# Loading two neighbouring tokens per piece in the first two batches of a gated-linear-attention and mixer kernel

## The chip, the cores and the metric

The kernel runs on one core of one Trainium2 chip. The metric is the device time of one launch in microseconds (us), the median over several runs.

A core has five engines that run side by side: TensorE (PE, matrix multiplies; its weight loads are shown as PEld), VectorE (DVE), ScalarE (ACT), GpSimd (POOL) and SyncE (SP, which here issues every transfer). They work on SBUF (128 partitions); PE writes its results to PSUM, which has eight banks of 128 x 512 fp32. Sixteen DMA engines carry data between HBM and SBUF. Each engine runs its own list of instructions in a fixed order, and semaphores make it wait for the others.

## What is computed

The reference chains two parts. The first is a recurrence with a gate per channel, for 4 batches, 8 heads, 768 tokens and head width 48:

```python
for t in range(S):
    state = alpha[:, :, t, :, None] * state + np.einsum('bhd,bhe->bhde', k[:, :, t], v[:, :, t])
    y[:, :, t] = np.einsum('bhd,bhde->bhe', q[:, :, t], state)
```

The heads of `y` are laid side by side to `x` (4 x 768 x 384), and a mixer follows: `U` is 768 x 32, `V` 32 x 768, `w_ch1` 384 x 1536 and `w_ch2` 1536 x 384.

```python
h = x.transpose(0, 2, 1) @ U @ V
u = x + h.transpose(0, 2, 1)
ch = np.maximum(u @ w_ch1, 0.0) @ w_ch2
return u + ch
```

Inputs and output are fp32 in HBM; the matmuls take bf16.

## The kernel before

**The recurrence in chunks.** A batch is cut into six chunks of 128 tokens. One chunk, all eight heads, is one call of `stage_gla` (L325). Tokens lie on the partitions. `stage_loads` (L313) brings four tiles of 128 x 8 x 48 fp32 for each chunk: alpha, k, q and v. In HBM a head's token is a row of 48 values, so that each load consists of 1024 pieces of 192 bytes:

```python
P.add({"SP": 1020.0}, lambda e: nc.sync.dma_start(t(), src[b, :, sl, :].rearrange("h t d -> t h d")), w=[t], prio=key)
```

Then, for each chunk:

- ScalarE takes the logarithm of alpha (`lt`, L331). PE multiplies it by an upper triangle of ones, which gives the prefix sums over the tokens (L338), and by a column of ones, which gives the totals (L341), with a mask added by `offd` (L339). ScalarE takes exp of minus, plus and total (`ai`, `aa`, `tot`, L349 to L351).
- `rk = k * ai` and `rq = q * aa` (L356, on POOL or DVE) are transposed by PE (L368) and copied from PSUM to `kT` and `qT`. `rv` is v in bf16.
- PE forms the scores of each head (L389, 48 rows of the array, so two heads at a time in 64-row tiles). VectorE multiplies them by the causal mask `maskc` into `pm` (L399).
- PE forms the state's increment `rk' rv` (L416). In the first batch PE also adds the state before, through an identity matrix (L414), and VectorE multiplies by `tot` (L427). In later batches VectorE adds (`sm`, L439), then POOL or VectorE multiplies.
- `y` is the state before seen through `qT` (L450) plus `pm' rv` (L452). It is copied to `xb`.

**The mixer.** After the six chunks of a batch, `stage_mix` (L461) forms `U' x` (L469) and from it `u = x + V' U' x` twice: as `uT`, with channels on the partitions (in the first batch directly, L488 and L491; later by transposing, L510), and as `ub`, with tokens on the partitions (L500 and the sum on VectorE, L501). `mlp1` (L525) multiplies `uT` by the first weights (L537, three matmuls for each of 24 tiles) with a relu (L547 on ACT, L549 on DVE). `mlp2` (L553) multiplies by the second weights (L560, twelve matmuls for each of 6 tiles), adds `ub` (L567) and stores (L568).

**What sets the order.** Nothing is ordered by hand. Every operation is handed to a planner (`Plan.add`) with an assumed cost for each engine that may do it, a priority and the tiles it reads and writes. `Plan.run` walks a clock of its own: at each step it takes, of the engines, the one that could start first, gives it the ready operation of lowest priority number, and hands out buffers and PSUM banks as they come free. The outcome is a fixed order for each engine. A `Buf` with a `reserve` takes a bank only when more than that many are free; `mlp1` and `mlp2` do so with 4 except in the last batch (L527, L554). `slack` is added to the time at which an operation counts as ready, and PE pays 95 ns in the plan for each change of tile mode. In the early part idle PE is given filler matmuls on zeros (L268), up to 33 us of the plan's clock.

Loads have priorities too. Chunk `kk`'s alpha, k and q have `kk`, `kk + 0.1` and `kk + 0.2`; v has `kk + 1.25`, that is behind alpha, k and q of the next chunk, except in the last chunk of a batch. The fp32 input ring `io` has 36 tiles; the 24 weight tiles pass through it too, twelve behind the loads of the first batch (priority 5.5) and twelve behind chunk 7 (7.9).

## Time and profile before

| What | Value |
|---|---|
| median of 5 runs | 181.38 us (180.14 to 182.75) |
| the profiled execution | 181.89 us, of which its span is 180.1 us |
| PE busy | 162.5 us (90% of the span) |
| DVE, ACT, POOL busy | 107.3, 103.4, 57.3 us |
| HBM read, written | 23.79 MB, 4.72 MB |
| DMA packets | 107603, of which 101408 under 512 bytes |
| loads of alpha, k, q, v | 24 each, 192 KB each, 3.7 to 3.9 us from issue to landing |
| weight loads | 24, 192 KB each, 4.4 us from issue to landing |

The span is the stretch from the first to the last recorded event of one execution. The profile page shows the busy share of each engine in 40 slices of the span; other views give the busy time in any stretch, the instructions in order of time with what each waited for, and the chain of work that ended last. A matmul's duration in the records (about 330 ns for 384 columns) includes the way through the array; matmuls that follow each other overlap, so that the pitch from one to the next is shorter.

### The profile page before, as it was taken

The numbers are of one execution on the slowest core, as the hardware profiler recorded it, in microseconds if no ns is written. First come the engines' busy times: TensorE is split into PE (matmuls) and PEld (weight loads), VectorE is DVE, ScalarE is ACT, GpSimd is POOL, SyncE is SP. The second block draws the span as 40 slices with busy tenths as digits, with TensorE's granted clock in tenths as the row PEclk, the third lists the DMA queues.
The fourth block names the chain that finished last, engine by engine and source line by source line (L and its number), as shares of the span: only waits on it lengthen the run. The fifth ranks groups of instructions, "written<-read, shape, count | busy, mean of one in ns | idle before, by whom it ended". The sixth has DMA issues, their size and how long they took to land.

```text
span 180.1 us, 4283 instructions
## 1 busy us (share of the span) xinstructions
PE 162.5 (90%) x1622; PEld 101.4 (56%) x1622; DVE 107.3 (60%) x209; ACT 103.4 (57%) x241; POOL 57.3 (32%) x90
## 2 busy tenths in 40 slices
PE   6778688889989998877999999999999999999992
PEld 2344455456556665454766576566665665665560
DVE  2486787969637895693789789376672822100331
ACT  4556558786775545693789759217867200897000
POOL 5432320225434664606584545424600000000000
PEclk9999999999999999996999999999999999999999
DMA  5999999999999998998999989881000023100222
GB/s 117 218 201 209 203 235 292 240 195 309 289 214 188 251 218 186 251 221 169 223 191 184 204 163 220 175 247 47 0 0 4 0 87 116 63 0 0 87 87 87
DMA packets 107603, 28.77 MB, mean 160 GB/s; under 512 B 101408, under 2 KB 107552, under 8 KB 107584
## 3 DMA queue, kind: packets, MB, share of 16 engines
q1 hardware_dynamic: 107584, 28.52, 69.6%
q8 instruction: 12, 0.20, 0.4%
q14 instruction: 7, 0.06, 0.1%
HBM read 23.79 MB, written 4.72 MB: 158 GB/s over the span
## 4 chain that ended last, share of the span: by engine, by line
PE 50%; SPq 16%; DMA 13%; issue 6%; DVE 5%; POOL 4%; ACT 4%; POOLq 0%; ACTq 0%
PE ps L560 20%; PE ps L537 19%; SPq L316 12%; DMA io<-in_alpha_dram 7%; DMA io<-in_moe_w_ch_dram 5%; SPq L294 3%; PE ps L368 3%; DMA out_dram<-ou 2%; DVE pm L399 2%; POOL rq L356 1%; POOL rk L356 1%; PE ps L452 1%; PE ps L338 1%; PE ps L389 1%; DVE rq L356 1%
## 5 line engine op out<-in xcount | busy, mean ns | idle before, releaser
L537 PE MATMUL ps<-uT,w_sb 128*128 128x384 bf16 x288 | 53.7, 331 | 0.4 <-ACT uT L275 0.4
L560 PE MATMUL ps<-w_sb,h1t 128*128 128x384 bf16 x288 | 50.1, 326 | 0.0
L547 ACT ACTIVATE h1t<-ps 128x384 bf16<-128x384 f32 x70 | 33.4, 490 | 21.3 <-PE ps L537 21.0
L560 PEld LDWEIGHTS <-h1t 128*128 128x128 bf16 x288 | 27.1, 98 | 16.5
L537 PEld LDWEIGHTS <-w_sb 128*128 128x128 bf16 x288 | 26.3, 98 | 16.3 <-issue 1.3
L399 DVE TENSOR_TENSOR pm<-ps,maskc 128x512 bf16<-128x512 f32 x48 | 31.0, 683 | 3.1 <-PE ps L389 3.1
L567 DVE TENSOR_TENSOR ou<-ub,ps 128x384 f32<-128x384 bf16 x24 | 13.3, 553 | 32.9 <-PE ps L560 31.3
L356 POOL TENSOR_TENSOR rk<-io,ai 128x384 bf16<-128x384 f32 x21 | 19.5, 928 | 24.9 <-ACT ai L349 22.2
L549 DVE TENSOR_SCALAR h1t<-ps 128x384 bf16<-128x384 f32 x26 | 13.8, 555 | 9.5 <-PE ps L537 9.4
L356 POOL TENSOR_TENSOR rq<-io,aa 128x384 bf16<-128x384 f32 x16 | 14.6, 913 | 8.5 <-PE ps L368 3.2
L331 ACT ACTIVATE lt<-io 128x384 bf16<-128x384 f32 x24 | 12.8, 532 | 7.4 <-DMA io<-in_alpha_dram 7.1
L349 ACT ACTIVATE ai<-ps 128x384 bf16<-128x384 f32 x24 | 12.0, 501 | 6.6 <-PE ps L341 4.9
L279 POOL CAST rv<-io 128x384 bf16<-128x384 f32 x18 | 9.8, 551 | 13.4 <-DMA io<-in_v_dram 10.0
L501 DVE TENSOR_TENSOR ub<-xb,ps 128x384 bf16<-128x384 bf16 x24 | 11.6, 548 | 3.1 <-PE ps L500 3.1
L368 PE MATMUL ps<-ident,rk 128*128 128x128 bf16 x96 | 9.6, 224 | 3.5 <-POOL rk L356 2.1
L350 ACT ACTIVATE aa<-ps 128x384 bf16<-128x384 f32 x24 | 12.1, 503 | 0.0
L268 PE MATMUL ps<-filler 128*128 128x512 bf16 x34 | 10.7, 423 | 1.2 <-DVE offd L235 1.2
L368 PE MATMUL ps<-ident,rq 128*128 128x128 bf16 x96 | 9.4, 220 | 2.3 <-POOL rq L356 1.9
L368 PEld LDWEIGHTS <-rk 128*128 128x128 bf16 x96 | 6.5, 100 | 8.0 <-POOL rk L356 4.3
L452 PE MATMUL ps<-rv,pm 128*128 128x48 bf16 x192 | 9.5, 185 | 1.6 <-DVE pm L399 1.6
L427 POOL TENSOR_TENSOR st<-sm,tot 128x384 bf16<-128x384 f32 x8 | 6.6, 829 | 13.3 <-DVE sm L439 13.3
L275 ACT COPY qt<-ps 128x512 bf16<-128x512 bf16 x12 | 7.1, 588 | 6.4 <-PE ps L368 4.8
(71 smaller groups left out, 198.3 us busy)
## 6 DMA issues: line engine op xcount, KB each, us to landing
io<-in_alpha_dram SPq DMA_DIRECT2D x24, 192.0 KB, 3.9
io<-in_k_dram SPq DMA_DIRECT2D x24, 192.0 KB, 3.9
io<-in_q_dram SPq DMA_DIRECT2D x24, 192.0 KB, 3.9
io<-in_v_dram SPq DMA_DIRECT2D x24, 192.0 KB, 3.7
io<-in_moe_w_ch_dram SPq DMA_DIRECT2D x24, 192.0 KB, 4.4
out_dram<-ou SPq DMA_DIRECT2D x24, 192.0 KB, 1.9
u_in<-in_moe_U_dram SPq DMA_DIRECT2D x1, 96.0 KB, 3.3
v_in<-in_moe_V_dram SPq DMA_DIRECT2D x1, 96.0 KB, 2.9
```

The source lines that it names most:

```text
L316: P.add({"SP": 1020.0}, lambda e: nc.sync.dma_start(t(), src[b, :, sl, :].rearrange("h t d -> t h d")), w=[t], prio=key)
L331: P.add({"ACT": 435}, lambda e: nc.scalar.activation(lt()[:, :, 0:D], at(), AF.Ln), r=[at], w=[lt], prio=pr + 40, slack=sl)
L349: P.add({"ACT": 390}, lambda e: nc.scalar.activation(ai().rearrange("t h d -> t (h d)"), cb()[:, 0:DM], AF.Exp, scale=-1.0), r=[cb], w=[ai ...
L350: P.add({"ACT": 390}, lambda e: nc.scalar.activation(aa().rearrange("t h d -> t (h d)"), cb()[:, 0:DM], AF.Exp), r=[cb], w=[aa], prio=pr + ...
L356: eng.tensor_tensor(dst()[:, :, 0:D], a(), x(), op=ALU.mult)
L368: nc.tensor.matmul(t[:, p, :], lhsT=ring()[:, 2 * p : 2 * p + 2, :].rearrange("t h w -> t (h w)"), rhs=ident, start=True, stop=True, is_tr ...
L399: nc.vector.tensor_tensor(pm()[:, :, par, :], s2, maskc.to_broadcast([C, HP, C]), op=ALU.mult)
L537: nc.tensor.matmul(hb()[:, 0:TW], lhsT=w1_sb[:, ct, jt * 128 : (jt + 1) * 128], rhs=uT()[:, ct, tt * TW : (tt + 1) * TW], start=(ct == 0), ...
L547: nc.scalar.activation(dst, hb()[:, 0:TW], AF.Relu)
L549: nc.vector.tensor_scalar_max(dst, hb()[:, 0:TW], 0.0)
L560: nc.tensor.matmul(hb()[:, 0:DM], lhsT=h1()[:, jt, c * C : (c + 1) * C], rhs=w2_sb[:, jt, :], start=(jt == 0), stop=(jt == NJ - 1),)
L567: P.add({"DVE": 468}, lambda e: nc.vector.tensor_tensor(ou(), ub()[:, c, :], hb()[:, 0:DM], op=ALU.add), r=[hb, (ub, c)], w=[ou], prio=-100)
```

## The change

Only batches 0 and 1 (`PAIR`) are treated in the new way. Their loads take two neighbouring tokens per piece: partition p of a tile holds tokens 2p and 2p+1 of a block of 256 tokens, for four of the eight heads. A load still has 192 KB, in 512 pieces of 384 bytes. A unit of work is then two chunks by four heads instead of one chunk by eight heads: partitions 0 to 63 belong to the first chunk of the block and 64 to 127 to the second, and a token's parity `j` takes the place of half of the heads in the free dimension. There are six units in a batch, as there were six chunks; two states run side by side, one for each half of the heads.

The new `stage_pair` does for a unit what `stage_gla` does for a chunk. The prefix sums take three matmuls (`upto` is the triangle within each chunk, `below` the same without its diagonal). The scores are 16 matmuls of 64 x 64 tiles, the state increments eight and the outputs sixteen matmuls in 64-row tiles. The copy of the transposed q puts the two parities back in the tokens' order. States, and the copies of y, are handled in halves of 192 columns. New constant tiles are built at the start.

Besides, in the whole kernel: `ub` of the first batch (L500, L501) has a later priority and reserves three banks; `mlp1` and `mlp2` reserve 2, 2, 2 and 0 banks; v of batches 2 and 3 has priority `kk + 0.3`; the plan's cost of a load is 720 or 900 instead of 1020; fillers end at 28 us of the plan's clock. `stage_gla` now serves batches 2 and 3 alone and loses its branches for the first two.

```diff
+    PAIR = (0, 1)
+    RES = (2, 2, 2, 0)
...
+    upto = const.tile([C, C], BF16, name="upto")
+    nc.vector.tensor_copy(upto, ut_ones)
+    nc.vector.memset(upto[0:64, 64:128], 0.0)
+    below = const.tile([C, C], BF16, name="below")
+    nc.vector.tensor_tensor(below, upto, ident, op=ALU.subtract)
+    mask2 = const.tile([C, 2, 2 * C], BF16, name="mask2")
+    nc.gpsimd.memset(mask2, 0.0)
+    nc.gpsimd.affine_select(
+        out=mask2, in_=mask2, compare_op=ALU.is_gt, fill=1.0, base=0, pattern=[[1, 2], [-1, 2 * C]], channel_multiplier=2
+    )
+    maskp = const.tile([C, 1, 2, C], BF16, name="maskp")
+    nc.vector.tensor_copy(maskp[0:64, 0], mask2[0:64, :, 0:C])
+    nc.vector.tensor_copy(maskp[64:128, 0], mask2[64:128, :, C : 2 * C])
...
-    P.warm_until = 33000.0
+    P.warm_until = 28000.0
...
+            if b in PAIR:
+                hs, sl = slice((c % 2) * HP, (c % 2 + 1) * HP), slice((c // 2) * 2 * C, (c // 2 + 1) * 2 * C)
+                P.add(
+                    {"SP": 720.0},
+                    lambda e: nc.sync.dma_start(
+                        t().rearrange("p (h j) d -> p h (j d)", j=2), src[b, hs, sl, :].rearrange("h (p j) d -> p h (j d)", j=2)
+                    ),
+                    w=[t], prio=key,
+                )
+                return
...
-            for t, src, o in ((at, alpha, 0.0), (kt, k, 0.1), (qt, q, 0.2), (vt, v, 1.25 if c < NC - 1 else 0.3)):
+            for t, src, o in ((at, alpha, 0.0), (kt, k, 0.1), (qt, q, 0.2), (vt, v, 1.25 if c < NC - 1 and b in PAIR else 0.3)):
...
+    def stage_pair(b, u, sprev, xb):
...
+        def f_cum(e):
+            l2 = jh(lt()[:, :, 0:D])
+            nc.tensor.matmul(cb()[:, 0:DM].rearrange("p (i h d) -> p i h d", i=2, d=D), lhsT=upto, rhs=l2[:, 0:1].to_broadcast([C, 2, HP, D]), start=True, stop=False)
+            nc.tensor.matmul(cb()[:, 0:Q], lhsT=below, rhs=l2[:, 1], start=False, stop=False)
+            nc.tensor.matmul(cb()[:, Q : 2 * Q], lhsT=upto, rhs=l2[:, 1], start=False, stop=False)
...
+        def f_ev(e, dst, tb, swap):
+            t = bf(tb())[:, 0:512].rearrange("x (a j m) -> x a j m", a=2, j=2)
+            d = dst().rearrange("x e c -> x (e c)")
+            d = d.rearrange("x (a m j) -> x a j m", a=2, j=2) if swap else d.rearrange("x (a j m) -> x a j m", a=2, j=2)
+            copy(e, d, t)
...
+        def f_sc(e):
+            for n in range(4):
+                a, j = n // 2, n % 2
+                for par in range(2):
+                    o = 64 * par
+                    for c in range(2):
+                        r = slice(64 * c, 64 * c + 64)
+                        nc.tensor.matmul(
+                            sc[par]()[r, n * C : (n + 1) * C],
+                            lhsT=kT()[o : o + D, n, r], rhs=qT()[o : o + D, 2 * a + c, :],
+                            start=(n == 0), stop=(n == 3), skip_group_check=True,
+                        )
+
+        P.add({"PE": mm(*[C] * 4)}, f_sc, r=[kT, qT], w=[sc[0], sc[1]], prio=pr + 10, mode="Q", slack=sl)
...
+        P.add({"PE": mm(*[2 * D] * 4)}, f_d, r=[rk, rv], w=db, prio=pr + 8, mode="H", slack=sl)
...
+        def f_y(e):
+            for h in range(HP):
+                for j in range(2):
+                    for c in range(2):
+                        r = slice(64 * c, 64 * c + 64)
+                        nc.tensor.matmul(
+                            yb[c]()[:, h * D : (h + 1) * D], lhsT=pm()[r, (h // 2) * 2 + j, h % 2, :], rhs=rv()[r, HP * j + h, :],
+                            start=(h == 0 and j == 0 and before[c] is None), stop=(h == HP - 1 and j == 1), skip_group_check=True,
+                        )
...
-            pr += 100.0
+            pr = mlp_prio(0, 0.3)
         for c in range(NC):
-            hb = Buf(bank)
+            hb = Buf(bank, 3 if b == 0 else 0)
...
-            hb = Buf(bank, 0 if b == B - 1 else 4)
+            hb = Buf(bank, RES[b])
...
-        st = None
+        st = [None, None]
         for c in range(NC):
-            st = stage_gla(b, c, st, xb)
+            if b in PAIR:
+                st[c % 2] = stage_pair(b, c, st[c % 2], xb)
+            else:
+                st[0] = stage_gla(b, c, st[0], xb)
```

## The prediction

> **What bounds the kernel now.** I read the busy rows of the page first, then the stretches between the events of the program, then the timeline at the places where TensorE (PE) waits.
>
> ```profile
> PE   6778688889989998877999999999999999999992
> PEclk9999999999999999996999999999999999999999
> DMA  5999999999999998998999989881000023100222
> ```
>
> Each digit is a slice of 4.5 us. The DMA engines are full up to slice 27 (122 us), when the last input has landed; PE has nines without a break from slice 19 (86 us) on. So two bounds follow one another, and both are full between 86 and 122 us. A busy PE is not a PE at its peak, so I count its work instead. The chain that ended last shows the pitch of one matmul where nothing waits:
>
> ```profile
> 142.16 11.05 PE ps L560 x68
> 153.21 11.70 PE ps L537 x72
> 164.91 11.71 PE ps L560 x72
> 120.09 0.33 PE ps L389 x8
> 120.42 1.41 PE ps L560 x8
> ```
>
> 11.70/72 gives 162.5 ns for a matmul of 384 columns (0.423 ns a column, so 56 ns for 128 columns, 42 for 96, 82 for 192). The eight score matmuls in 64-row mode (L389) cost 0.33 us plus 0.11 us by which the eight matmuls after them exceed 8 x 162.5 = 1.30: 0.44 us, of which 8 x 26 ns are matmuls and 0.23 us the way into the mode and back, so 0.115 us a switch. L452 (48 columns) takes 25 ns each (0.20 us for 8 in the same chain). With these prices the PE queue of the program before holds 146.4 us of work without the fillers of L268. The stretches:
>
> ```profile
> core 0: us, PE busy (x) PEld busy (x) DVE busy (x) ACT busy (x) POOL busy (x), PEclk, DMA share, GB/s
> 4.00:36.60 32.60, 25.09 (x296) 14.40 (x296) 24.36 (x46) 20.44 (x51) 8.51 (x11) 1.00 1.02 227
> 36.60:70.00 33.40, 32.41 (x346) 21.21 (x345) 23.29 (x43) 21.82 (x55) 15.58 (x23) 1.00 1.00 234
> 70.00:86.00 16.00, 12.10 (x145) 7.79 (x140) 10.49 (x21) 9.89 (x24) 6.77 (x9) 0.90 1.01 212
> 86.00:122.00 36.00, 35.70 (x407) 23.68 (x405) 28.44 (x53) 22.73 (x55) 18.85 (x25) 1.00 0.94 198
> 122.00:177.00 55.00, 54.48 (x433) 33.45 (x431) 19.55 (x37) 26.84 (x58) 5.18 (x6) 1.00 0.12 44
> ```
>
> Up to 36.66 us (first prefix-sum matmul of batch 1) my count of real PE work is 15.9 us: 20.8 us are idle or filler. From there to 70.07 us (the same matmul of batch 2) it is 32 us of 33.4. From 70 to 86 us it is 9.3 us of 16, and the clock drops. From 86.03 to 176.65 us, where the last matmul ends, it is 89.2 us of 90.6. So PE's own work sets the end, and what can be gained is its idle time before 86 us, which DMA causes:
>
> ```profile
> 69.50 0.52 ACT L331 ACTIVATE lt<-io 128x384 bf16<-128x384 f32 x1 [0.60 <-DMA io<-in_alpha_dram]
> 70.07 0.33 PE L338 MATMUL ps<-lt,ut_ones 128*128 128x384 bf16 x1
> 81.65 0.51 POOL L279 CAST rv<-io 128x384 bf16<-128x384 f32 x1 [4.70 <-DMA io<-in_v_dram]
> 82.21 0.29 PE L416 MATMUL ps<-rv,rk 128*128 128x96 bf16 x3 [1.99 <-POOL rv L279]
> ```
>
> The first load of batch 2 starts its chunk at 69.5 us; at 81.65 us a late v holds PE for 2 us, and the 90% clock of that stretch follows.
>
> **The change, part by part.**
>
> *Loads.* 48 of the 96 input loads move 512 pieces of 384 bytes in place of 1024 of 192. The price of a piece, from stretches of one kind:
>
> ```profile
> 4.00:24.00 20.00, 14.94 (x190) 8.63 (x191) 13.57 (x26) 11.33 (x30) 6.59 (x8) 1.00 1.06 206
> 26.00:34.00 8.00, 6.78 (x79) 4.21 (x80) 6.28 (x12) 6.32 (x15) 0.35 (x1) 1.00 0.99 296
> 41.00:49.00 8.00, 7.84 (x75) 4.82 (x74) 6.79 (x13) 5.29 (x14) 4.38 (x8) 1.00 0.96 306
> ```
>
> 192 KB at 206 GB/s is 0.954 us for a load in 192-byte pieces; at 300 GB/s it is 0.655 us in the weights' 1536-byte pieces. The trace has no 384-byte piece. Bounds: 0.954 (no gain) and 0.655. A straight line through the two, per piece and engine (14.9 and 82 ns), gives 24.5 ns x 32 = 0.784 us. A rule of the Trainium skill speaks against the change: "DMA: Bandwidth & Descriptors", section Specifications, asks for at least 512 bytes for line rate and says that below this the engine reads, modifies and writes; 384 is still below, which taken at its worst leaves 0.954. The same page, "How a descriptor splits into AXI transactions", has reads start at 256-byte boundaries: 192-byte pieces at multiples of 192 then fetch 9 beats of 32 bytes on average, 384-byte pieces 14, so 7 for each 192; with its 3 cycles a packet that is 12 against 8.5, an estimate of 0.676 us. I take 0.73, between line and page: 0.224 us x 48 = 10.75 us of DMA, half of it in batch 0. Under the 512-byte rule it is nothing. The SP queue has the same 148 instructions, but three output stores that stood ahead of the first load of batch 2 come later: 3 x 0.655 = 2.0 us. First load of batch 2: 69.5 - 12.75 = 56.8 us, and its prefix sum can run at 57.4.
>
> *v of the last two batches.* Its place goes from one chunk late to its own chunk. That removes the wait of 4.7 us at 81.65; it pulls each v ahead of the next chunk's alpha by one load (about 1 us), which costs nothing while DMA is ahead of PE, as it then is.
>
> *PE work of a pair unit* (12 units take the place of 12 chunks). Prefix sum: two more matmuls of 192 columns, +0.165 us. Scores: 16 of 64x64 in place of 8. The trace has no 64x64 tile; perfect overlap of four would be 14 ns each, the nearest row (L452) says 25 each, and I take 25: 0.40 against 0.21, +0.19. State increments: 8 of 64 rows at 25 against 4 at 42, +0.03. Outputs: 16 at 25 against 8, +0.20. Identity matmuls: 8 of 192 columns against 4 of 384, even. Switches: 96 in the whole queue against 59, 37 x 0.115 = 4.3 us. Sum: 12 x 0.585 + 4.3 = 11.3 us; PE's queue grows from 146.4 to 157.6. The "TensorEngine Tiling (Array Packing)" page of the skill, Restrictions, says that column tiling disables the fast weight load; by "TensorE: Matmul & The Clock Gate" (LDWEIGHTS) 64 columns then take 53 ns, so 0.85 us for 16 and +5.4 us over 12 units. The column-tiled loads that the trace has speak against it:
>
> ```profile
> 72.46 0.12 PEld L469 LDWEIGHTS <-u_sb 128*32 128x32 bf16 x6
> ```
>
> Six in 0.12 us. I stay with 25 ns; with the rule only the two score groups that stand behind the point below would show fully, +0.9 us.
>
> *Order: the first batch's sums later.* This decides what 11.3 us are worth. I counted the PE queue up to the first prefix sum of batch 2. Before: 47.8 us ahead of it, 98.6 behind, and all 72 second-layer matmuls of batch 0 (11.7 us) ahead. After: 43.8 ahead, 113.8 behind, and those 72 all behind. The pair units' extra work thus falls nearly all ahead of that point, beside loads that PE waits for anyway, and the work moved behind fills 70 to 86 us, where PE stood still. If that cover is gone, each us of it counts in full.
>
> *VectorE, ScalarE, GpSimd.* The swapped copy of q's transposes writes in steps of two elements; not in the trace: 0.42 us (plain copy on VectorE) to 0.68 (the masks' fp32 pass of 512), I take 0.60. State and y operations come in halves; a half has no row here, between 0.28 (half of 0.55) and 0.55, I take 0.35. The masks stay two of 0.64 (1.28 for two). VectorE's queue from batch 0's transposed sums to batch 1's last mask, at pitches of the timeline (1.49 us for 3 relus, 2.87 for 6 sums): 13 relus x 0.50, 12 masks x 0.64, 13 state halves x 0.35, 6 sums x 0.48, 4 scalings x 0.70, 3 swapped and 2 plain copies, 4 y halves: 28.4 us, some 25 ahead of the point. The densest stretch of the trace has VectorE busy 8.9 of 10 us, so 25 us need 28.1. ScalarE has less there. The new constants (a 128x512 select on GpSimd, about 4 x 0.29, then copies on VectorE) delay batch 0's first mask and padding by up to 1 us, beside loads.
>
> *Sum.* Batch 1's first prefix sum: 36.66 - 24 x 0.224 = 31.3 us. The first of batch 2 comes at the latest of three: PE 31.3 + (43.8 - 19.5 of work) = 55.6; DMA 57.4; VectorE 31.3 + 28.1 = 59.4. I take 58.5. Behind it 113.8 us, plus idle at the rate of today's dense part (1.4 in 89) 1.8: last matmul at 174.1 against 176.65, -2.55 us. The profiled execution took 181.89 us (span 180.1 and 1.8 around it), so 179.3; the median of the five runs, 181.38, lies 0.5 under it: 178.8 us.
>
> **Rivals.** (1) *VectorE becomes the bound in batch 1.* My sum leaves 27 us for batch 1 up to that point, with 25 us of VectorE work in them. Break-even is a first prefix sum of batch 2 at 61.05 us (176.65 - 115.6), 2.5 us behind my value. If VectorE reaches only the 79% of 86 to 122 us (28.44 of 36), 25 us take 31.6 and the point is 62.9, and a us more if the swapped copy waits too: 64, end at 179.6, +2.95, 184.3 us. For it: no stretch is denser than 89%. Against: ScalarE may take copies, and batch 0 ran at 75%. (2) *384 bytes are no cheaper* (the 512-byte rule): only 2 us of stores move, point at 68.1, end 183.7, 188.4 us. Against: the weights' 300 GB/s show that pieces cost. (3) *The loads run ahead but the gain is paid back*: point at 60.5 to 61.5, no change, 181.4. (4) *Loads at 0.68 and PE alone binding*: point at 56.2, end 171.8, 176.5 us.
>
> **How the numbers follow.** About 1% (1.8 us) is what a measurement of this kernel tells from no change. Chances: my forecast 0.45 (range 176.5 to 181, of it 0.09 within 1%), rival 4 0.14, rival 3 0.15, rival 1 0.19, rival 2 0.07. Faster 0.36 + 0.14 = 0.50, same 0.24, slower 0.26. The range, 175.5 to 184.5, leaves out rival 2 and the far ends of 1 and 4.
>
> **What would show it.** A load rate of 260 to 290 GB/s in the first 20 us (206: rival 2). The first prefix sum of batch 2 near 58 us and no PE gap of over 1 us after it; a VectorE busy above 8.5 of 10 between 31 and 60 with PE waiting for masks is rival 1. Score groups of 16 in about 0.6 us; 0.9 or more means slow weight loads. The forecast falls if that prefix sum comes behind 61 us or if the work behind it takes clearly more than 116 us.

## The result: no change, and the profile after

The changed kernel takes 181.38 us (median of 36 runs, 180.41 to 184.32) against 181.2 us (median of 71) for the kernel before, measured beside it: ratio 1.0022, 95% interval 1.0004 to 1.004. That is no change, where 178.8 us was forecast.

The profiled execution took 183.32 us (span 181.2 and 2.1 around it; before, 1.8 around it). It is one of the slow ones of this kernel, as those profiled of e9 and e13 are of theirs, so that its end lies 1.9 us behind that of a median one. The waits below return in e1 to e3, whose queues differ by one or two places, at spans of 178 to 179 us.

The busy rows of the changed kernel, one digit for a slice of 4.5 us:

```profile
PE   6997885799999899984999999999999999999992
PEclk9999999699999999997899999999999999999998
DMA  5999999899997899999999998112000121200222
```

DMA stays full up to 113 us (the 25th slice) in place of 122 us: input is complete some 9 us earlier. TensorE's nines should have begun earlier too. They do, with the 9th slice, but the 19th (81.5 to 86 us) has a 4, and the clock is 0.7 and 0.8 in the two slices from there. The stretches of the changed kernel (the columns are named in the first line):

```profile
core 0: us, PE busy (x) PEld busy (x) DVE busy (x) ACT busy (x) POOL busy (x), PEclk, DMA share, GB/s
4.00:24.00 20.00, 17.69 (x304) 11.16 (x303) 14.73 (x47) 13.98 (x37) 9.38 (x15) 1.00 1.13 259
24.00:36.00 12.00, 8.22 (x108) 5.02 (x105) 5.47 (x11) 7.95 (x18) 2.97 (x5) 0.88 0.96 274
58.00:70.00 12.00, 11.42 (x195) 7.33 (x193) 11.25 (x21) 7.46 (x21) 6.87 (x10) 1.00 1.03 182
70.00:86.00 16.00, 12.81 (x121) 8.44 (x120) 7.80 (x16) 5.71 (x12) 5.16 (x8) 0.95 1.04 197
86.00:112.00 26.00, 26.00 (x277) 16.74 (x275) 16.45 (x31) 16.66 (x40) 11.37 (x16) 0.97 1.12 204
```

The first row answers the question of price: 192 KB at 259 GB/s are 0.76 us a load (0.954 before). From 58 us on, with the plain 192-byte loads of batches 2 and 3, the rate is 182 and then 197 GB/s: 192 KB take 1.08 and then 1.00 us. The first store is issued only here:

```profile
68.66 2.31 SPq L776 DMA_DIRECT2D out_dram<-ou  x1
```

So the stores do not explain the 182; what does stays open.

From 70 to 86 us TensorE stands still for 3.2 us, all in one place. First that place in the timeline of all engines, then GpSimd's own timeline ahead of it:

```profile
82.16 0.52 ACT L543 ACTIVATE lt<-io 128x384 bf16<-128x384 f32 x1 [3.48 <-DMA io<-in_alpha_dram]
82.59 0.47 ACT L561 ACTIVATE ai<-ps 128x384 bf16<-128x384 f32 x1
83.14 0.91 POOL L568 TENSOR_TENSOR rk<-io,ai 128x384 bf16<-128x384 f32 x1 [1.12 <-ACT ai L561]
84.11 0.41 PE L624 MATMUL ps<-rv,rk 128*128 128x96 bf16 x4 [3.19 <-POOL rk L568]
```

```profile
71.43 0.50 POOL L298 CAST rv<-io 128x384 bf16<-128x384 f32 x1 [2.82 <-DMA io<-in_v_dram]
71.89 0.83 POOL L635 TENSOR_TENSOR st<-sm,tot 128x384 bf16<-128x384 f32 x1
75.39 0.50 POOL L298 CAST rv<-io 128x384 bf16<-128x384 f32 x1 [2.66 <-DMA io<-in_v_dram]
81.52 0.51 POOL L298 CAST rv<-io 128x384 bf16<-128x384 f32 x1 [5.63 <-DMA io<-in_v_dram]
83.14 0.91 POOL L568 TENSOR_TENSOR rk<-io,ai 128x384 bf16<-128x384 f32 x1 [1.12 <-ACT ai L561]
```

Read upward from TensorE. It waits for `rk` of chunk 2 (the third) of batch 2, which needs `ai`. On ScalarE `ai` stands behind the logarithm of chunk 5, which waits 3.48 us for its alpha. On GpSimd the same `rk` stands behind three copies of v, of its own chunk and of the next two, which wait 11 us together for their loads. Neither the logarithm nor the copies are needed for `rk`: each engine keeps to its list, and the list put work that needs a later load ahead of work whose data are long there.

Two single events of the timeline, the first prefix sum of batch 2 and the end of the chain:

```profile
58.96 0.32 PE L550 MATMUL ps<-lt,ut_ones 128*128 128x384 bf16 x1
```

```profile
166.01 11.71 PE ps L768 x72
177.75 0.56 DVE ou L775
```

So that prefix sum came 11.1 us earlier than before (70.07), as forecast, and the last matmul 1.1 us later than before (177.7 against 176.65). Between them lie 118.8 us where 115.6 were forecast; in e1 to e3 it is 116.8 to 118.1.

### The profile page after: what moved, and what is told of

Its sections match the earlier page's. It is cut to its first block, busy times and chain, and to the rows that moved or that the text cites. A ratio compares the mean times of both kernels' runs of the same rounds, so it can differ in the third digit from the quotient of the medians.

```text
span 181.2 us, 4818 instructions
## 1 busy us (share of the span) xinstructions
PE 166.1 (92%) x1864; PEld 104.9 (58%) x1864; DVE 107.8 (60%) x226; ACT 105.1 (58%) x249; POOL 64.3 (35%) x101
## 4 chain that ended last, share of the span: by engine, by line
PE 70%; SPq 13%; DMA 6%; DVE 4%; issue 3%; POOL 1%; ACT 0%; POOLq 0%; DVEq 0%
PE ps L745 26%; PE ps L768 23%; SPq L338 9%; DMA io<-in_moe_w_ch_dram 3%; PE ps L580 3%; SPq L313 3%; DMA io<-in_v_dram 3%; PE ps L601 2%; PE ps L708 2%; PE ps L718 1%; PE ps L414 1%; PE ps L660 1%; PE ps L624 1%; PE ps L699 1%; PE ps L550 1%
## 5 line engine op out<-in xcount | busy, mean ns | idle before, releaser
L775 DVE TENSOR_TENSOR ou<-ub,ps 128x384 f32<-128x384 bf16 x24 | 13.2, 552 | 31.5 <-PE ps L768 31.3
L611 DVE TENSOR_TENSOR pm<-ps,maskc 128x512 bf16<-128x512 f32 x24 | 15.5, 686 | 6.5 <-PE ps L601 6.3
L452 DVE TENSOR_TENSOR pm<-ps,maskp 128x512 bf16<-128x512 f32 x24 | 15.7, 679 | 1.7 <-PE ps L441 1.7
L568 POOL TENSOR_TENSOR rk<-io,ai 128x384 bf16<-128x384 f32 x12 | 11.1, 923 | 11.2 <-ACT ai L561 8.0
L543 ACT ACTIVATE lt<-io 128x384 bf16<-128x384 f32 x12 | 6.4, 535 | 14.8 <-DMA io<-in_alpha_dram 11.4
L294 ACT CAST xb<-ps 128x192 bf16<-128x192 f32 (+1 forms) x23 | 8.8, 394 | 6.8 <-PE ps L660 6.7
L294 ACT COPY kt<-ps 128x512 bf16<-128x512 bf16 x15 | 8.7, 588 | 5.1 <-PE ps L580 3.8
L294 ACT COPY qt<-ps 128x512 bf16<-128x512 bf16 x15 | 10.0, 664 | 3.0 <-PE ps L580 1.4
L568 POOL TENSOR_TENSOR rq<-io,aa 128x384 bf16<-128x384 f32 x12 | 11.6, 963 | 0.0
L294 ACT CAST w_sb<-io 128x384 bf16<-128x384 f32 x15 | 7.3, 512 | 2.9 <-DMA io<-in_moe_w_ch_dram 2.9
L394 ACT ACTIVATE ai<-ps 128x384 bf16<-128x384 f32 x12 | 5.9, 491 | 5.1 <-PE ps L387 4.2
L287 PE MATMUL ps<-filler 128*128 128x512 bf16 x16 | 6.9, 533 | 1.2 <-DVE filler L223 1.2
```

The lines of the kernel that those rows point to most:

```text
L294: nc.scalar.copy(dst, src)
L452: nc.vector.tensor_tensor(dst, s2, maskp.to_broadcast([C, 2, 2, C]), op=ALU.mult)
L568: eng.tensor_tensor(dst()[:, :, 0:D], a(), x(), op=ALU.mult)
L611: nc.vector.tensor_tensor(pm()[:, :, par, :], s2, maskc.to_broadcast([C, HP, C]), op=ALU.mult)
L775: P.add({"DVE": 468}, lambda e: nc.vector.tensor_tensor(ou(), ub()[:, c, :], hb()[:, 0:DM], op=ALU.add), r=[hb, (ub, c)], w=[ou], prio=-100)
```

## The experiments

Each ratio is to the kernel before, run beside it on the same chip. "Gap" is idle time of TensorE ahead of one group. Idle from 58 to 112 us is read from the stretches (before: 0.09 + 3.90 + 0.11 = 4.1 us; changed: 0.58 + 3.19 = 3.8 us).

**One hold on ScalarE, and an early copy (e1, e2, e3).** My first theory saw only the ScalarE queue. After the planner has made its order, e1 moves the logarithm of chunk 5 behind the exponentials of chunk 2 (the line with `ln` below), e2 the copy of weights behind the copy of batch 0's `utx` (the last three), and e3 both (`...` marks lines left out, here and below):

```
+        def later(x, y):
+            i, j = order.index(x), order.index(y)
...
+            order.insert(j, order.pop(i))
+        later(next(o for o in order if o.tag == ("ln", 2, 5)), next(o for o in order if o.tag == ("tot", 2, 2)))
+        u = next(o for o in order if o.tag == ("utx", 0))
+        act = [o for o in order if o.eng == "ACT"]
+        later(act[act.index(u) - 1], u)
```

> The changed kernel with one instruction of ScalarE's queue moved: the logarithm of chunk 5 of batch 2, which waits for its alpha until 82.16 us, now stands behind the three exps of chunk 2 instead of ahead of them. Every other queue is as it was. Theory (a wait at the head of ScalarE's queue holds the exps, GpSimd's scaling and PE, 3.2 us, and the clock falls after it): the gap of PE at 81 to 84 us is gone, the end comes 3 to 5 us earlier, 176.5 to 178.5 us, ratio to the kernel before 0.975 to 0.985. Rival (PE waits there for loads in any case, or the work behind is late for its own reasons): under 1 us, ratio 0.998 to 1.003.

> The changed kernel with one instruction of ScalarE's queue moved: the copy of batch 0's U'x (utx) now stands ahead of the weight copy that waits for its load until 31.99 us. Theory (the same sort of wait held PE for 2.5 us at 30.5 to 32.9 us and the clock fell for 5 us): batch 1's first prefix sum comes at 31 to 33 us instead of 35.1. Whether the end moves depends on what comes after: VectorE is busy 9.7 of 10 us between 50 and 60 us, so if VectorE or the loads set the first prefix sum of batch 2 (58.96 us) the end stays within 1 us (ratio 0.996 to 1.003); if that prefix sum only followed from the late start, the end comes 2 to 4 us earlier (ratio 0.98 to 0.99).

> Both moves together in the changed kernel. Theory (the forecast was right up to the first prefix sum of batch 2 and lost its gain to the wait at 82 us): 176 to 178 us, ratio 0.97 to 0.985, and it is the first move that does it. Rival (the gain was never there): ratio 0.995 to 1.003.

| | ratio (95%) | first prefix sum of batch 2 | last matmul ends | gaps on rk |
|---|---|---|---|---|
| e1 | 1.0113 (1.0055 to 1.017) | 57.9 | 176.0 | 2.0 at 81 us, 2.3 at 95 us |
| e2 | 1.0061 (1.0031 to 1.0091) | 58.5 | 175.3 | 3.0 at 82.6, 0.6 at 94.5 |
| e3 | 1.0065 (1.0022 to 1.0109) | 57.7 | 174.8 | 1.5 at 80.3, 1.8 at 94 |

None is faster, by the ratios. In e1 the gap shrank to 2.0 us and one of 2.3 us came up two chunks later. GpSimd's timeline of e1 shows why:

```profile
79.56 0.51 POOL L308 CAST rv<-io 128x384 bf16<-128x384 f32 x1 [5.07 <-DMA io<-in_v_dram]
80.03 0.91 POOL L578 TENSOR_TENSOR rk<-io,ai 128x384 bf16<-128x384 f32 x1
```

With the logarithm out of the way, `rk` still stands behind a copy that waits 5.07 us for v. The theory of a single hold fell. Here is the dense part of e2:

```profile
70.00:86.00 16.00, 13.01 (x135) 8.54 (x133) 8.43 (x17) 7.45 (x16) 5.33 (x8) 1.00 1.08 218
86.00:112.00 26.00, 25.40 (x293) 16.71 (x291) 17.40 (x34) 17.13 (x42) 12.43 (x17) 1.00 0.96 192
```

From 58 to 112 us TensorE idles for 4.7, 4.0 and 3.7 us in e1, e2 and e3, at a full clock. So the waits return without the lower clock that the changed kernel's profile shows behind 70 us (0.95 and 0.97); it does not recur even behind e2's gap of 3.0 us. Batch 1 began 1.5 to 2.6 us ahead of the 35.07 us of the changed kernel in all three (in e1 without the move of e2 too); batch 2 then began 0.5 to 1.2 us earlier, and the time did not fall.

**What the pieces are worth (e4).** The loads of batches 0 and 1 as 1024 pieces of 192 bytes, all queues unchanged:

```
-                hs, sl = slice((c % 2) * HP, (c % 2 + 1) * HP), slice((c // 2) * 2 * C, (c // 2 + 1) * 2 * C)
+                sl = slice(c * C, (c + 1) * C)
...
-                        t().rearrange("p (h j) d -> p h (j d)", j=2), src[b, hs, sl, :].rearrange("h (p j) d -> p h (j d)", j=2)
...
+                    lambda e: nc.sync.dma_start(t(), src[b, :, sl, :].rearrange("h t d -> t h d")),
```

> The changed kernel with all queues as they were, but the loads of batches 0 and 1 again take eight heads of 128 tokens in 1024 pieces of 192 bytes, as before the change; the tiles then hold other tokens than the units take them for, so what is computed is another sum of the same size. It measures the worth of the longer pieces alone. Theory (0.76 us a load against 0.954, 48 loads): first 20 us at about 206 GB/s instead of 259, first prefix sum of batch 2 at 66 to 69 us instead of 59, and the end 6 to 10 us later than the changed kernel: 187 to 191 us, ratio 1.03 to 1.055. Rival (VectorE and PE set that prefix sum, loads were hidden): within 2 us of the changed kernel, ratio 1.00 to 1.012.

Ratio 1.0897 (1.0804 to 1.099). The stretch of e4 at the start:

```profile
4.00:24.00 20.00, 16.27 (x215) 10.70 (x217) 11.42 (x38) 11.36 (x29) 7.79 (x13) 0.92 1.27 189
```

189 GB/s against 259, and the first prefix sum of batch 2 at 71.5 us against 59.0; 206 GB/s, 66 to 69 us and a ratio of 1.055 at most were expected. In this order of the queues the larger pieces bring 12.6 us, and without them the program is 9% slower than before. Not all of that need be the price of the pieces: the order was written for loads of 0.72 us, and e4 runs it with loads of 1.04 (192 KB at 189 GB/s) and a lower clock.

**Are the loads of batch 2 late, or is the order wrong? (e5, e6, e7, e8).** e5 gives batches 2 and 3 the same 384-byte pieces, with every queue as it was. e6 changes only what the planner believes a plain load costs. e7 undoes the place of v. e8 keeps the pairs, with the price of 720 for their loads, and takes back all the other scheduling edits. What e5 computes is, as in e4, another sum of the same size.

```
e5
-            P.add({"SP": 900.0}, lambda e: nc.sync.dma_start(t(), src[b, :, sl, :].rearrange("h t d -> t h d")), w=[t], prio=key)
+            hs, sl = slice((c % 2) * HP, (c % 2 + 1) * HP), slice((c // 2) * 2 * C, (c // 2 + 1) * 2 * C)
...
+                {"SP": 900.0},
...
+                    t().rearrange("p (h j) d -> p h (j d)", j=2), src[b, hs, sl, :].rearrange("h (p j) d -> p h (j d)", j=2)
...
e6 (and e8)
-            P.add({"SP": 900.0}, lambda e: nc.sync.dma_start(t(), src[b, :, sl, :].rearrange("h t d -> t h d")), w=[t], prio=key)
+            P.add({"SP": 1020.0}, lambda e: nc.sync.dma_start(t(), src[b, :, sl, :].rearrange("h t d -> t h d")), w=[t], prio=key)
e7 (and e8), in the table of loads
-(vt, v, 1.25 if c < NC - 1 and b in PAIR else 0.3)
+(vt, v, 1.25 if c < NC - 1 else 0.3)
e8
-    RES = (2, 2, 2, 0)
+    RES = (4, 4, 4, 0)
-    P.warm_until = 28000.0
+    P.warm_until = 33000.0
-            pr = mlp_prio(0, 0.3)
+            pr += 100.0
-            hb = Buf(bank, 3 if b == 0 else 0)
+            hb = Buf(bank)
```

> The changed kernel with the 48 loads of batches 2 and 3 in 384-byte pieces too; every queue keeps its order, and what these two batches compute is another sum of the same size (tokens and heads of a tile change places). Theory A (TensorE waits in batch 2 because its loads land only as fast as TensorE uses them up: about 1.0 us a load between 58 and 110 us): loads of batch 2 land at 0.76 us a piece, its second half about 4 us earlier; the gaps of 3.2 us at 81 to 84 us and the drop of the clock behind them are gone, TensorE's idle time between 58 and 112 us falls from 3.8 to under 1.5 us, the last matmul comes 115 us or less behind the first prefix sum of batch 2, time 178 (ratio to the kernel before 0.98 to 0.99). Theory B (the order of the queues, written for loads of 0.9 us, holds TensorE, whatever the loads do): the gaps stay within 1 us of 3.2. Theory C (TensorE's own work behind the point was counted too small): gaps gone and the last matmul still 118 us behind the point, time 181.

> The changed kernel with the plain loads' cost in the planner put back from 900 to 1020 ns; nothing else. Theory B (order written for loads that land sooner than they do): copies of v and logarithms stand later in their queues, the gap of 3.2 us at 81 to 84 us falls under 1 us without a new one over 1 us behind it, time 178 to 179.5. Theory A (the loads themselves are late): the gaps only move; idle between 58 and 112 us stays at 3 to 4.5 us, time within 1% of the changed kernel.

> The changed kernel with v of batches 2 and 3 loaded one chunk late again, as before the change. If pulling v ahead of the next alpha is what holds the exponentials' chain in batch 2 (my step that this costs nothing fails): the wait of a product behind alpha goes, 2 to 3 us are saved, time 178.5 to 179.5. If the loads are simply behind: the wait passes over to the copy of v (as in the kernel before, 4.7 us at 81.65), idle between 58 and 112 us stays at 3 to 5 us, time within 1% of the changed kernel.

> Pairs and 64-row units alone: the first batch's sums, the reserves of PSUM, the planner's price of a load, v's place and the end of the warm-up as in the kernel before. If the later sums are what fills 70 to 86 us with work (as forecast): the first prefix sum of batch 2 comes later than 59 us by 3 to 6 us because 11.7 us of second-layer matmuls and VectorE's six sums stand ahead of it again, and less work is behind it; idle of over 4 us between there and 90 us; time 183 to 186. If the order of these sums does not matter because loads set the middle anyway: time 181 within 1%.

e5: ratio 0.9637 (0.9552 to 0.9722), 176.6 us, more than Theory A had. Its stretches from 58 us, and the ends of its way behind the point:

```profile
58.00:70.00 12.00, 12.00 (x193) 7.72 (x192) 10.23 (x21) 7.12 (x22) 7.90 (x11) 1.00 1.05 262
70.00:86.00 16.00, 16.00 (x168) 10.75 (x165) 10.19 (x20) 10.65 (x24) 7.07 (x10) 1.00 1.03 272
86.00:112.00 26.00, 26.00 (x300) 17.18 (x299) 18.16 (x35) 17.32 (x45) 13.69 (x18) 1.00 0.46 114
```

```profile
57.57 0.32 PE L556 MATMUL ps<-lt,ut_ones 128*128 128x384 bf16 x1 [0.50 <-ACT lt L549]
158.69 11.71 PE ps L774 x72
```

262 and 272 GB/s, no idle time at all, and the last matmul 112.9 us behind the first prefix sum of batch 2. The same order of all queues is a good one when a load takes 0.72 to 0.75 us and a bad one when it takes 1.0 to 1.08. Theory A holds, and C (TensorE's own work counted too small) falls.

e6: ratio 0.9842 (0.9738 to 0.9945), 180.7 us where before took 183.4 on that chip. No gap of 1 us is left behind 58 us (the largest 0.92 and 0.73), and idle from 58 to 112 us is 2.5 us. So theory B holds as well: the two are one mismatch between the loads and an order written for faster ones, and it can be repaired from either side, here in part.

e7: 1.0101 (1.007 to 1.0131), within 1% of the changed kernel. Idle from 58 to 112 us is 6.0 us. The largest gap, 2.6 us at 103 us, is again one on `rk`, and again `rk` stands behind a copy of v that waited 2.85 us for its load. v's late place is no cure under a price of 900.

e8: 1.0545 (1.0433 to 1.0657), far more than my 183 to 186 us. The prefix sum of batch 2 came at 60.4 us, 1.4 later and not 3 to 6, and none of batch 0's 72 second-layer matmuls stands ahead of it, as in the changed kernel; the loss is idle time of 4.6 us between 36 and 58, 3.5 between 86 and 112 (3.1 of it one wait for a logarithm behind its alpha at 99 us), and clocks of 0.75 and 0.87. Its last matmul ended at 188.3 us.

**The other half alone, more pairs, other prices (e9 to e12).**

```
e9, on the kernel before (the new lines)
+    P.warm_until = 28000.0
+            P.add({"SP": 900.0}, lambda e: nc.sync.dma_start(t(), src[b, :, sl, :].rearrange("h t d -> t h d")), w=[t], prio=key)
+(vt, v, 1.25 if c < NC - 1 and b < 2 else 0.3)
+            pr = mlp_prio(0, 0.3)
+            hb = Buf(bank, 3 if b == 0 else 0)
+            hb = Buf(bank, (2, 2, 2, 0)[b])
e10, on e6
-    PAIR = (0, 1)
+    PAIR = (0, 1, 2)
e11, on e6
-    PAIR = (0, 1)
+    PAIR = (0, 1, 2, 3)
e12, on the changed kernel (the new line)
+            P.add({"SP": 1100.0}, lambda e: nc.sync.dma_start(t(), src[b, :, sl, :].rearrange("h t d -> t h d")), w=[t], prio=key)
```

> The kernel before (192-byte pieces, plain chunks) with the change's scheduling alone: first batch's sums later, reserves of 2 banks, load price 900, v of batches 2 and 3 in its own chunk, warm-up to 28 us. If the later sums only pay when loads run ahead: TensorE has no loads to work on when the sums leave, the first prefix sum of batch 2 stays within 1.5 us of 70, set by the loads, with more work behind it: time 184 to 190. If the later order is a gain by itself (it fills TensorE's idle time between 70 and 86 us, 6.7 us of it without work before): time 177 to 179.

> The changed kernel with the planner's load price at 1020 and pairs of tokens for batch 2 as well. Theory A (in batch 2 the loads are what TensorE waits for) gives: 24 loads of batch 2 at 0.76 in place of about 1.0 us, no idle over 1 us between 58 and 112 us; six pair units more cost some 0.7 us each (switches 0.3, prefix sum 0.17, scores, state and output 0.2), 4 us, nearly all of it in TensorE's dense stretch: net between 1 us faster and 2 us slower than the same with two batches (e6, ratio 0.984 to before): 0.98 to 0.995. If pair units cost TensorE as much as my forecast had (0.94 us with switches): 5.6 us, ratio 0.995 to 1.005.

> The same with pairs in all four batches. Loads end some 10 us earlier, which serves nothing behind 112 us, where TensorE has no idle time; 12 pair units more cost 8 us of TensorE's work in the dense stretch: ratio to before 1.00 to 1.02, slower than with three. If the loads still bound the time there: ratio 0.97 to 0.98.

> The changed kernel with the planner's price of a plain load at 1100 in place of 900 ns (its trace has 0.96 to 1.1 us for one between 58 and 86 us). Theory B (the order must not run ahead of the loads): as with 1020, gaps under 1 us between 58 and 112 us, ratio to before 0.975 to 0.99. If the gain at 1020 was a chance order: 0.995 to 1.01, with a gap of 2 us or more in that stretch again.

e9: 1.0003 (0.9972 to 1.0035), outside both expectations. The first prefix sum of batch 2 came when it came before (70.07 us), and the last matmul 0.7 us later (177.3):

```profile
70.06 0.34 PE L338 MATMUL ps<-lt,ut_ones 128*128 128x384 bf16 x1
```

Of batch 0's 72 second-layer matmuls 60 still stand ahead of it. So scheduling alone neither moves that point nor puts those sums behind it: with pairs they go behind it with (the changed kernel) or without (e8) the scheduling edits. Scheduling alone changes nothing, pairs alone cost 5.5%, both together 0.2%: the parts do not add. My reading is that pairs need an order that fits them.

e10: 1.0087 (1.0059 to 1.0114); e11: 1.0323 (1.0249 to 1.0398), both above their expectation. Against e6 the last matmul comes 1.95 and 5.7 us later (175.5, 177.4, 181.2). The units add work in TensorE's dense part, by these ends some 0.3 to 0.5 us each. The ratios lie further from e6 (2.5 and 4.9%) than the ends do; they were taken on another chip, and the rest was not followed.

e12: 0.9756 (0.9716 to 0.9796), 176.8 us, without a gap of 0.5 us behind 58 us.

**By hand or by price, and what belongs to the change (e13 to e18).** e13 moves copies of v on GpSimd behind `rq` of earlier chunks (the first four of the pairs below, each moved behind its second), e14 also the logarithm of e1 (the fifth). e15 and e17 put the price (1020 in the kernel before) to 1100 and 1200 in the same line as e6 does, e16 and e18 put 1200 into the changed kernel.

```
+MOVES = [
+    (("rv", 2, 4), ("rq", 2, 2)),
+    (("rv", 2, 3), ("rq", 2, 2)),
+    (("rv", 2, 5), ("rq", 2, 3)),
+    (("rv", 3, 1), ("rq", 2, 4)),
+    (("ln", 2, 5), ("tot", 2, 2)),
+]
```

> The changed kernel (load price 900) with four copies of v on GpSimd moved behind products of earlier chunks of batch 2: v of chunks 3 and 4 behind rq of chunk 2, v of chunk 5 behind rq of chunk 3, v of chunk 1 of batch 3 behind rq of chunk 4; nothing else moves. If these copies, which stand ahead of rk and wait for v, are the second hold beside the logarithm of chunk 5 on ScalarE: alone they leave the ScalarE wait, the gap at 81 to 84 us falls from 3.2 to about 2.5 us, time within 1% of the changed kernel. If GpSimd's queue alone was the hold: gap under 1 us, last matmul 2 to 3 us earlier, ratio to before 0.98 to 0.99.

> The same with the logarithm of chunk 5 of batch 2 moved behind the exponentials of chunk 2 as well (the move of e1). If the two queues held rk together, each alone enough: gap at 80 to 84 us under 1 us, last matmul 115.5 us or less behind the first prefix sum of batch 2, idle of TensorE between 58 and 112 us under 2 us, ratio to before 0.98 to 0.99. If the gain of the load price (e6, e12) came from the split of TensorE's work ahead and behind, and not from these queues: the gap goes, but time stays within 0.5% of before.

> The kernel before with its own load price put from 1020 to 1100 ns: a control for e12. If the price only repairs what the change's 900 spoiled: within 1% of before. If 1100 is a better price for this planner whatever the pieces: ratio 0.97 to 0.985.

> The changed kernel with a load price of 1200: a third point beside 1020 (0.984) and 1100 (0.976). If the mechanism is that work which waits for loads must not stand ahead of work which could run: ratio 0.97 to 0.99 again, gaps under 1 us between 58 and 112 us. If 1100 was a lucky order: 0.995 or more.

> The kernel before with a load price of 1200 in place of 1020. If the planner's price is worth as much without the change (1100 gave 0.985): ratio to before 0.97 to 0.99. If the price gains only where loads run ahead: 0.99 to 1.01.

> The changed kernel with a load price of 1200 once more, beside the kernel before with the same price (e17) on one chip. If the change gains what was forecast (some 2.5 us) once its queues do not run ahead of the loads: 0.01 to 0.02 below the ratio of e17, at 0.97 to 0.98. If the price alone makes the gain: within 0.005 of e17.

| price of a plain load | kernel before | changed kernel |
|---|---|---|
| 900 | (e9, with the other scheduling edits) 1.0003 | 1.0022 (1.0004 to 1.004) |
| 1020 | 1 (as it is) | e6 0.9842 (0.9738 to 0.9945) |
| 1100 | e15 0.9854 (0.9796 to 0.9912) | e12 0.9756 (0.9716 to 0.9796) |
| 1200 | e17 1.0166 (1.0126 to 1.0206) | e16 0.9734 (0.9691 to 0.9776), e18 0.9745 (0.9704 to 0.9787) |

e15 fell on the side of "a better price whatever the pieces"; e17 fell outside both of its expectations; e18 lies further below e17 than the 0.01 to 0.02 expected.

e13 alone left the gap at 3.0 us (about 2.5 expected), as ScalarE's logarithm holds too; ratio 0.9965 (0.9933 to 0.9997). In e14 that gap is gone, so each of the two holds was enough alone. But the ratio is only 0.9967 (0.9943 to 0.9991), not 0.98 to 0.99: the outcome that its expectation had put down to the split of TensorE's own work. TensorE's timeline of e14 has the next gaps, GpSimd's what stands before the second:

```profile
85.91 0.34 PE L645 MATMUL ps<-rv,rk 128*128 128x96 bf16 x4 [1.14 <-POOL rk L589]
99.04 0.40 PE L601 MATMUL ps<-ident,rk 128*128 128x128 bf16 x4 [1.76 <-POOL rk L589]
```

```profile
97.61 0.50 POOL L319 CAST rv<-io 128x384 bf16<-128x384 f32 x1 [3.11 <-DMA io<-in_v_dram]
98.08 0.91 POOL L589 TENSOR_TENSOR rk<-io,ai 128x384 bf16<-128x384 f32 x1
```

Idle from 58 to 112 us is still 3.6 us, so e14 does not decide between the two. Five moves clear one place, and waits return at later chunks: the second again behind a copy of v, the first behind a logarithm that the trace has waiting for TensorE.

The price moves all of these places, and TensorE's own order too. In e12 and e16 the first prefix sum of batch 2 comes later than at 900 (61.6 and 60.5 us), and the way behind it is only 110 us, also because 8 second-layer matmuls and some work of the last pair units now stand ahead of it. The engine waits for nothing there:

```profile
60.45 0.33 PE L550 MATMUL ps<-lt,ut_ones 128*128 128x384 bf16 x1
```

GpSimd in e16, at the place shown above:

```profile
70.86 0.92 POOL L568 TENSOR_TENSOR rk<-io,ai 128x384 bf16<-128x384 f32 x1
71.73 0.92 POOL L568 TENSOR_TENSOR rq<-io,aa 128x384 bf16<-128x384 f32 x1
75.04 0.51 POOL L298 CAST rv<-io 128x384 bf16<-128x384 f32 x1 [2.39 <-DMA io<-in_v_dram]
80.22 0.51 POOL L298 CAST rv<-io 128x384 bf16<-128x384 f32 x1 [4.68 <-DMA io<-in_v_dram]
```

The copies wait as long as ever (4.68 us), but `rk` is done before them, and the stretches of e16 show that TensorE misses nothing:

```profile
24.00:36.00 12.00, 9.55 (x127) 6.08 (x127) 7.18 (x15) 10.01 (x24) 4.52 (x8) 1.00 1.04 298
58.00:70.00 12.00, 12.00 (x192) 7.71 (x192) 9.93 (x21) 6.36 (x18) 5.46 (x8) 1.00 0.95 188
70.00:86.00 16.00, 16.00 (x173) 10.79 (x169) 12.25 (x24) 9.86 (x23) 6.01 (x9) 1.00 1.01 218
86.00:112.00 26.00, 25.86 (x300) 17.27 (x299) 18.93 (x38) 17.71 (x44) 15.13 (x21) 1.00 1.07 190
```

The loads are as slow as in the changed kernel (188 to 218 GB/s), the idle time is 0.14 us, and the last matmul ends at 170.9 us against 177.7. That is 6.8 us between the two profiles; by the ratios the difference is 5.2 us. The stretches account for most of the 6.8: idle time from 58 to 112 us (3.8 against 0.1), the clock there (12.81 x 0.05 + 26 x 0.03 = 1.4 us), and the work done from 24 to 36 us, busy time times clock (8.22 x 0.88 = 7.2 against 9.55 us, so 2.3 us), less 1.0 us more idle in e16 between 36 and 58 us: 6.4 us. The clock's 1.4 us do not recur in e1 to e3. How much of the rest is order on GpSimd and ScalarE, and how much order on TensorE, these runs do not separate.

With its best price of those tried the changed kernel takes 176.1 us (e16, e18), the kernel before 178.2 (e15). The change is then worth 0.9734/0.9854 = 0.988, both on one chip: some 1.2%, with intervals that do not overlap. At equal prices the differences are 1.0% at 1100 (the two intervals just touch) and 4.2% at 1200, where the kernel before turns worse again. No smooth rule ties the price to the time: a price is also a draw of an order, worth 1 to 2% either way. The version to keep is the changed kernel with 1200.

## Why the prediction was wrong, step by step

*Price of a load*: 0.73 us forecast, 0.76 measured, of the bounds 0.655 and 0.954. The Trainium skill's rule of 512 bytes ("DMA: Bandwidth & Descriptors", Specifications), read as no gain below it, is not what this chip did (259 GB/s with 384 bytes, 182 to 206 with 192). The estimate of 0.676 us from the same page was too low; the 3 cycles a packet in it stand there under "Why small descriptors are slow (HBM only)". This step was right; in this order of the queues e4 is 8.7% slower.

*First prefix sum of batch 1*: 31.3 forecast, 35.07 measured, 32.5 to 33.6 in e1 to e3. In the profiled execution the copy of `utx` stood behind a copy of weights that waited 2.37 us for its load, and the clock fell (0.88 from 24 to 36 us); in e1, with the same order there, that copy did not wait, and the point came 2.6 us earlier. So most of the delay is no property of the order. It mattered little: batch 2's point was set elsewhere.

*First prefix sum of batch 2*: 58.5 forecast, 58.96 measured, 57.7 to 58.5 in e1 to e3. The number was right, but the sum did not yield it: by its own rule, the latest of three, it should have been VectorE's 59.4, and 58.5 lay between that and DMA's 57.4. In e1 to e3 TensorE waits there for the logarithm; in e1 this waits for its alpha:

```profile
57.31 0.52 ACT L553 ACTIVATE lt<-io 128x384 bf16<-128x384 f32 x1 [1.07 <-DMA io<-in_alpha_dram]
57.89 0.32 PE L560 MATMUL ps<-lt,ut_ones 128*128 128x384 bf16 x1 [0.73 <-ACT lt L553]
```

There the load set the point. VectorE was as close to the bound as rival 1 said, 9.67 of 10 us busy from 50 to 60 us in the changed kernel, without passing it.

*A pair unit on TensorE*. The chain of the changed kernel gives the groups:

```profile
39.65 0.28 PE ps L475 x8
39.93 0.59 PE ps L745 x3
43.46 0.35 PE ps L441 x16
43.81 1.08 PE ps L745 x6
44.89 0.30 PE ps L524 x16
45.19 1.57 PE ps L745 x9
```

Read as the forecast read its 0.44 us for eight scores, each group holds its way into the mode, and the group behind it the way out (1.08 - 6 x 0.1625 = 0.105 us). Sixteen scores then cost 0.455 us with both ways, hardly more than eight did: the tiles of 64x64 run side by side, near the 14 ns each that I had named as perfect overlap and not taken. Outputs cost 0.41 (0.20 before), the state 0.38 (0.17 before), the prefix sum 0.165 more. That is some 0.6 us more for a unit, switches included, where the forecast had 0.94: too dear, but nearly all of it ahead of the point, where loads set the pace. The slow weight load of column tiling (the Trainium skill, "TensorEngine Tiling (Array Packing)", Restrictions) does not show in the time of the group.

*The work moved behind the point "fills 70 to 86 us, where PE stood still"*, with *1.8 us of idle time behind the point* and *v in its own chunk "costs nothing while DMA is ahead of PE, as it then is"*: **these failed.** The work itself was counted well: 118.8 us less 3.8 of idle time and 1.4 of lower clock leave 113.6, and e1 to e3 less their idle time 112.8 to 113.4, where 113.8 was forecast. The idle time was not: it is 3.8 us from 58 to 112 us (3.7 to 4.7 in e1 to e3), hardly different from the 4.1 of the kernel before, where the rate of the old dense part gave 1.8.

DMA was not ahead. I had worked out that loads would lead at the first prefix sum of batch 2 and took the lead for granted behind it, though the plain loads (1.0 to 1.08 us there, 0.954 in my sum) still came one by one until 112 us, and the work moved behind the point is no shield when the queues put waiting work ahead of it. The load price of 900, which my sum did not weigh, wrote an order for loads that land sooner than they do. It was neither v's place by itself (e7) nor one queue (e1, e13), but the order against the loads it got (e5 from the side of the loads, e6, e12 and e16 from that of the order). Of the 4.0 us from 179.3 to the 183.3 of the profiled execution, 2.0 are idle time, 1.4 the clock, 0.5 the point and 0.3 the ends around the span, less 0.2 of work; the clock did not recur in e1 to e3. The median, 181.38, lies 2.6 us above the 178.8.

*The rivals.* The third (paid back, 181.4 us) had the time right with another mechanism: the point was not late, the way behind it was. The first did not occur, the second was excluded by 259 GB/s, the fourth by 0.76 us a load. My own two marks of failure, a gap over 1 us behind the point and clearly more than 116 us of work there, both appeared.

Freed of the waits by a price of 1200, the program ends at 170.9 us, below the 174.1 I had worked out. But part of that step is the price's own, as e15 shows, and the 1.2% that the change is worth with the best price on both sides is near the forecast 1.4% (178.8 against 181.38) in another order than the one forecast.

## What to carry to other kernels

When loads get faster in one stage, ask of every queue in the next one what stands at its head: an operation that waits for a late load holds everything behind it, and one wait removed by hand only shows the next. Where a planner writes the order, a price in it is part of the program: after a change of the transfers set it by the measured pitch of a load in the stage where it counts, or somewhat above, and try two or three values, since each is a new order. Test parts of a change together with the order that fits them; alone they may cost what they save in company.

## What the runs showed of the hardware

- Loads of one kind are not of one price: 192-byte pieces went at 206 GB/s in the first 20 us of the kernel before, at 182 to 204 in the changed one from 58 us on, and at 189 in the first stretch of e4. Stores are not what lowers it to 182: the first is issued at 68.66 us. What sets the difference was not tried.
- A lower clock need not cost anything: e16 and e18 are one program, with a granted clock of 1.00 and 0.74 from 24 to 36 us, and their last matmuls end at 170.9 and 171.0 us. In that stretch e18 does 0.9 us less of work (busy 11.69 us x 0.74 against 9.55), and it makes this up by 58 us, where e16 idles for 1.1 us and e18 for 0.04.
- Tiles run side by side: sixteen score matmuls of 64x64 tiles cost with both switches 0.455 us and eight in 64-row tiles 0.44. Sixteen matmuls of 48 columns in 64-row tiles took 0.30 us with the way in, 19 ns each, less than the 25 ns at which I had the shortest.
